# Second part's weight operands made in the products' ring of buffers, and first attention blocks with two rounds between scores and transposes

## The chip, the core and the metric

The kernel runs on one core of a Trainium2 chip. TensorE multiplies matrices into PSUM, VectorE (DVE), ScalarE (ACT) and GpSimd (POOL) work elementwise, and SyncE (SP) issues nearly all DMAs from one queue in order. Every engine runs its own instructions in order and waits on semaphores. The metric is the device time of one execution in microseconds; lower is better.

## What is computed

The data are fp32, except the second part's weights, which come in 64 bits and are turned to fp32 by the kernel. Attention over chunks of 64 tokens is followed by a mixture of four dense two-layer networks weighted by domain probabilities, and that by a gated layer. From the reference:

```python
scores = scale * np.matmul(q_c, k_c.transpose(0, 1, 2, 4, 3))
attn = softmax(scores)                       # per chunk of 64; 4 x 8 heads x 576 tokens x 64
x = heads side by side                       # 2304 tokens x 512
for e in range(4):                           # first part ("one"), w1 512x1024, w2 1024x512
    out += p[:, e:e + 1] * (np.maximum(x @ w1[e], 0.0) @ w2[e])
g = x @ w_gate                               # second part ("two"), 512x1536
return (g * (1 / (1 + np.exp(-g))) * (x @ w_val)) @ w_out
```

## The kernel before

**Split operands.** Each fp32 operand is kept as a high half, rounded by ScalarE, and a low half, the difference, made by VectorE or GpSimd (`split`). A product is three matmuls: high by high, high by low, low by high.

**Sets and products.** Layer 1 is cut into *sets*: a pair of 128-wide weight blocks in each direction against a pass of 768 tokens, done with seven products instead of eight (`PRODUCTS`, `product`). The seven products need sums of weight blocks (`w_sums`, four sums) and sums of x blocks. There are 48 sets of the first part (three passes of 16), then 36 of the second. The counter `now` counts products; one product is a *slot*. A slot holds six matmuls of layer 1 and the share of layer 2 of the group before (`layer2`, `gather` adds the result in VectorE). Three accumulators x, z and w are used: the products 0, 2, 4 and 6 add into x, and ScalarE copies the intermediate state out as `p` (after product 0) and `u` (after product 2) before the next product may add (`keep`).

**Weights of the first part.** Sets 2 to 17 split their operands from raw weights (`make_w`) into a ring of twelve buffers, pool `w`, and store them; later passes load them seven slots ahead (`load_w`).

**Weights of the second part.** While the first part's sets 18 to 47 run, generators make the second part's operands and store them in DRAM: `make_set64` converts two halves of a set (`convert`, from 64 bits to fp32: a ScalarE step `top`, six VectorE steps, one add of GpSimd, spread over slots by `yield`), makes the four sums in VectorE and splits seven operands, one a slot, into pool `made`, which has two buffers. `make_wo` does one block of the output weights. `run_tasks(2)` steps two generators once in a slot; the list `make64` gives two sets, then two blocks of output weights, and so on. A split's store is put off by two slots (`later(2, ...)`). The order of instructions is the order in which the code issues them.

**Opening.** Six blocks of attention run through four stages (scores, transpose, values, out), one block a round, each stage one round behind the one before. The first two sets are done as eight plain pieces (`plain`) between the last rounds and after them; `first_sums` makes the sums of x, `make_w` the operands of set 2, `split_w2` those of layer 2.

Of the kernel before, what the change touches and what calls it, by code (L numbers as in the profile page):

```python
# [10 lines left out]
F32 = mybir.dt.float32  # L11
# [8 lines left out]
P = 128  # L20
B, H, S, D = 4, 8, 576, 64
CH = 64
# [50 lines left out]
def attention_moe_gated(  # L73
# [141 lines left out]
    def att_scores(a, where):  # L215
        s = att[a]
        ps = att_ps(f"s{a}", where)
        for i in range(NPAIR):
            for c in range(2):
                b = slice(64 * c, 64 * c + 64)  # L220
                nc.tensor.matmul(
                    ps[b, 2 * i : 2 * i + 2], s["q"][:, i, b], s["k"][:, :, i, c], start=True, stop=True
                )
        if a + 2 < NS:
            att_load(a + 2)
        mx = st_p.tile([P, H], F32, tag="mx", name=f"mx{a}")
        e = s["e"] = at_p.tile([P, H, CH], F32, tag="e", name=f"e{a}", bufs=3)
        nc.vector.tensor_reduce(out=mx, in_=ps, op=ALU.max, axis=AX.X)
        nc.vector.tensor_tensor(out=e, in0=ps, in1=mx.unsqueeze(2).to_broadcast(ps.shape), op=ALU.subtract)
        nc.scalar.activation(e, e, AF.Exp, scale=SCALE)  # L230
# [40 lines left out]
    def att_out(a, where):  # L271
        ps = transpose(att_ps(f"xt{a}", where), att.pop(a)["e"]).rearrange("p (i c) k -> p i (c k)", c=2)
        s, b = divmod(a, BLOCKS)
        half, b = divmod(b, HALF)
        if s == 0:


            r = slice(b * P, (b + 1) * P)
            ops = [x_slots(0, f"b{i + 1}1") if half == 0 else x_slots(0, ("t4", "b22")[i]) for i in range(2)]
            for i, (h, _) in enumerate(ops):  # L280
                nc.scalar.activation(h[:, :, r], ps[:, 2 * i : 2 * i + 2], AF.Copy)
            for i, (h, l) in enumerate(ops):
                sub(l[:, :, r], ps[:, 2 * i : 2 * i + 2], h[:, :, r].bitcast(F32))
            t = x_first[half, b] = acc_p.tile([P, KD, P], F32, tag="acc", name=f"x0_{a}")
            nc.scalar.copy(t, ps)
        else:
            xb = at_p.tile([P, NPAIR, P], F32, tag="xb", name=f"xb{a}", bufs=1)
            nc.scalar.copy(xb, ps)
            nc.sync.dma_start(xs[s][half, :, :, b * P : (b + 1) * P], xb)

    def first_sums(j):

        b1, b2 = x_first[0, j], x_first[1, j]
        t = raw2_p.tile([P, KD, P], F32, tag="raw2", name=f"t12_{j}")
        r = slice(j * P, (j + 1) * P)
        d0, d1 = slice(0, 2), slice(2, 4)

        def part(b, src, lo=None):
            h, l = x_slots(0, b)
            split(h[:, :, r], l[:, :, r], src, lo)  # L300

        sub(t[:, d0], b2[:, d0], b1[:, d0])
        sub(t[:, d1], b2[:, d1], t[:, d0])
        sub(b2[:, d0], b2[:, d1], b2[:, d0], nc.gpsimd)
        part("t2", t[:, d1])
        part("t1", t[:, d0])
        part("t3", b2[:, d0], nc.gpsimd)
        sub(b1[:, d1], b1[:, d1], t[:, d1], nc.gpsimd)
# [67 lines left out]
    def make_set64(q, m):  # L376
        r = raw1_p.tile([P, 8, 2 * P], F32, tag="raw1", name=f"raw_{q}_{m}")
        for half in range(2):
            dst = r[:, 2 * half : 2 * half + 2].rearrange("p b f -> p (b f)")
            yield from convert(dst, (wg, wv)[m][q, half], f"{q}_{m}_{half}")  # L380
        w_sums(r)
        yield
        for i in range(NPROD):
            a = PRODUCTS[i][1]
            t = made_p.tile([P, 2, 2 * P], F32R, tag="made", name=f"made_{q}_{m}_{a}")
            split(t[:, 0], t[:, 1], r[:, a], lo=nc.gpsimd)
            later(2, lambda i=i, t=t: nc.sync.dma_start(w_d[NPAIRS + 2 * q + m][i], t.bitcast(F32)))
            yield

    def make_wo(c):  # L390
        t = made_p.tile([P, 512], F32, tag="made", name=f"made_wo_{c}")
        yield from convert(t, wo[c], f"wo_{c}")
        yield
        nc.sync.dma_start(wo_d[c], t)
        yield
# [177 lines left out]
    with tc.manual_schedule():  # L573
# [32 lines left out]

        spare = [(psA, "a"), (psA, "a"), (psX, "x"), (psX, "x"), (psY, "y"), (psY, "y")]
        count = [0]  # L610

        def where():
# [2 lines left out]

        ORDER = (A11, A12, A21, A22)
        pieces = [(n, c, t) for t in range(2) for n in range(2) for c in range(2)]
        zw = ("z", "w")
        for i in range(BLOCKS + len(STAGES) - 1):
            for d, stage in reversed(list(enumerate(STAGES))):  # L620
                if 0 <= i - d < BLOCKS:
                    stage(i - d, where())
            if i == 1:
                fetch_w1(1)
            if i in (2, 3):
                for a in ORDER[2 * i - 4 : 2 * i - 2]:
                    wplain[0, a] = w_split(raw1[0], a, 0)
            if i in (4, 5):
                for a in ORDER[2 * i - 8 : 2 * i - 6]:
                    wplain[1, a] = w_split(raw1[1], a, 1)  # L630
            if i >= BLOCKS - 1:
                plain(*pieces.pop(0), zw[i % 2])
            if i == BLOCKS:
                fetch_w2(0, 0)
                fetch_w2(0, 1)

        sm = t_p.tile([P, NS], F32, tag="sum", name="prob_sum", bufs=3)
        nc.vector.tensor_reduce(out=sm, in_=prob, op=ALU.add, axis=AX.X)
        nc.vector.tensor_scalar_add(sm, sm, EPS)
        nc.vector.reciprocal(sm, sm)  # L640
        nc.vector.tensor_tensor(out=prob, in0=prob, in1=sm.unsqueeze(2).to_broadcast(prob.shape), op=ALU.mult)
        raw1.clear()
        fetch_w1(2)
        fetch_w1(3)
        split_w2(0, 0)
        split_w2(0, 1)
        fetch_w2(0, 2)
        fetch_w2(0, 3)
        split_w2(0, 2)
        split_w2(0, 3)  # L650
        plain(*pieces.pop(0), "z")
        first_sums(0)
        w_sums(raw1[2])
        make_w(2, 0)
        plain(*pieces.pop(0), "w")
        first_sums(1)
        make_w(2, 1)
        plain(*pieces.pop(0), "z")
        first_sums(2)
        make_w(2, 2)  # L660
        plain(*pieces.pop(0), "w")
        for i in range(3, NPROD):
            make_w(2, i)
        for j in range(HALF):
            first_last(j)


        rest = []
# [7 lines left out]

        make64 = []
        for q in range(NPAIRS2):
            make64 += [make_set64(q, 0), make_set64(q, 1), make_wo(2 * q), make_wo(2 * q + 1)]

        def run_tasks(n):
            while len(running) < n and tasks:
# [10 lines left out]
        for n in range(FIRST, len(sets)):  # L693
# [3 lines left out]
            if group_of(n) != G:  # L697
# [1 line left out]
                first = now[0]  # L699
                slots = NPROD * sum(group_of(k) == G for k in range(len(sets)))  # L700
                two, taken = layer2(G - 1), 0
            if n + 2 < len(sets) and n + 2 > 3 and is_raw(n + 2):
                fetch_w1(n + 2)
            if n == N1:
                assert not tasks and not running, (len(tasks), len(running))
# [2 lines left out]
            for i in range(NPROD):  # L708
# [29 lines left out]
                if rest and i % 3 != 2:  # L738
                    stage, a = rest.pop(0)
                    stage(a, (psA, "a"))  # L740
                    if not rest:
# [1 line left out]
                        xt_p = ctx.enter_context(tc.tile_pool(name="xt", bufs=3, side="right"))  # L743
                        sums_p = ctx.enter_context(tc.tile_pool(name="sums", bufs=1, side="right"))
                        raw64_p = ctx.enter_context(tc.tile_pool(name="raw64", bufs=2, side="right"))
                        made_p = ctx.enter_context(tc.tile_pool(name="made", bufs=2, side="right"))
                        tasks.append(x_sums(1))
                if n == NPAIRS + 1 and i == NPROD - 1:
                    tasks += [x_sums(2)] + make64
# [73 lines left out]
```

## Time and profile before

| | |
|---|---|
| median of three runs | 1353.57 us (1349.45 to 1357.07) |
| the profiled execution: time, span | 1354.29 us, 1352.5 us |
| TensorE busy | 1281.5 us (95%) |
| VectorE, ScalarE, GpSimd busy | 754.3, 516.8, 551.7 us |
| mean granted TensorE clock | 0.981 |

An engine's busy time in a stretch is less than the stretch when it waited; "idle before" names what ended the wait. The granted clock is 1 at 2.4 GHz and 0.5 at 1.2 GHz, so 0.97 is a mean over both levels. A matmul's own duration overlaps the next one's, so the distance between starts is its cost.

### The profile page before, as it was taken

The page shows a single profiled execution, that of the slowest core. Times are in us where ns is not written, and L with a number is a line of the kernel's source. Part 1 is how long each engine was busy: PE and PEld are TensorE (multiplying, and loading weights), DVE is VectorE, ACT ScalarE, POOL GpSimd, SP SyncE. Part 2 cuts the span into 40 slices and gives each one's busy share as a digit, 9 for nine tenths or more (in the row PEclk, how much of TensorE's full clock was granted, in tenths as well). Part 3 has the DMA queues.
Part 4 walks back from the last instruction along what each step waited for, and adds up shares of the span by engine and source line. Part 5 has one row for each costly group of instructions (what it writes and reads, how often), then busy time and mean ns, then how long its engine had stood idle before and what let it go on. Part 6 is the DMA issues. An engine that isn't in the chain of part 4 may idle for free.

```text
span 1352.5 us, 19817 instructions
## 1 busy us (share of the span) xinstructions
PE 1281.5 (95%) x6724; PEld 1141.2 (84%) x6724; DVE 754.3 (56%) x1246; ACT 516.8 (38%) x1105; POOL 551.7 (41%) x527
## 2 busy tenths in 40 slices
PE   7899999999999989889898888999999999999998
PEld 6788888888987879778797777889999899989997
DVE  5665555556467867678458366544435433453343
ACT  3544444445433333343332333243334333343331
POOL 2543343567353353453443335242536323252331
PEclk9899999999999999999999898999999999999999
DMA  6286676676886767686884755665887666567651
GB/s 203 79 265 219 205 217 193 209 243 221 258 279 225 250 222 261 198 285 239 278 295 158 246 193 201 231 228 173 279 271 241 217 226 202 168 226 250 187 170 47
DMA packets 166885, 296.16 MB, mean 219 GB/s; under 512 B 17776, under 2 KB 43632, under 8 KB 166784
## 3 DMA queue, kind: packets, MB, share of 16 engines
q1 hardware_dynamic: 166752, 294.85, 65.7%
q8 instruction: 54, 0.88, 0.3%
q14 instruction: 47, 0.39, 0.1%
q0 software_dynamic: 32, 0.04, 0.0%
HBM read 219.84 MB, written 74.97 MB: 218 GB/s over the span
## 4 chain that ended last, share of the span: by engine, by line
PE 37%; DMA 7%; DVE 7%; issue 3%; ACT 3%; POOL 2%; SPq 0%; ACTq 0%; DVEq 0%; POOLq 0%
PE y L521 5%; PE y L517 5%; PE y L519 5%; PE lx L470 4%; PE lx L472 4%; PE lx L471 4%; DMA w<-made 4%; PE lz L470 2%; PE lz L471 2%; PE lz L472 2%; POOL made L106 1%; PE lw L472 1%; PE lw L471 1%; PE lw L470 1%; DMA raw_wo<-wo 1%
## 5 line engine op out<-in xcount | busy, mean ns | idle before, releaser
L106 POOL TENSOR_TENSOR w<-raw,w 128x512 fp32r<-128x512 f32 (+1 forms) x252 | 270.8, 1089 | 488.9 <-ACT w L105 418.2
L517 PE MATMUL y<-w,hh 128*128 128x512 f32 x792 | 315.5, 398 | 15.2 <-DVE acc L545 13.8
L521 PE MATMUL y<-w,hl 128*128 128x512 f32 x792 | 315.9, 399 | 2.3 <-DVE hl L428 2.3
L519 PE MATMUL y<-w,hh 128*128 128x512 f32 x792 | 314.8, 397 | 0.0
L517 PEld LDWEIGHTS y<-w,hh 128*128 128x128 f32 x792 | 150.6, 190 | 37.3 <-DVE acc L545 18.6
L521 PEld LDWEIGHTS y<-w,hl 128*128 128x128 f32 x792 | 150.9, 191 | 23.1 <-DVE hl L428 2.7
L519 PEld LDWEIGHTS y<-w,hh 128*128 128x128 f32 x792 | 150.4, 190 | 17.3
L105 ACT ACTIVATE w<-raw 128x512 fp32r<-128x512 f32 (+1 forms) x252 | 124.8, 522 | 11.2 <-DMA raw<-w 11.2
L458 DVE TENSOR_TENSOR sum_p<-lw,p 128x384 f32<-128x384 f32 x82 | 45.5, 555 | 149.3 <-PE lw L472 133.2
L427 ACT ACTIVATE hh<-sum_p 128x384 fp32r<-128x384 f32 x92 | 48.1, 523 | 193.2 <-DVE sum_p L458 193.0
L458 DVE TENSOR_TENSOR sum_p<-lx,p 128x384 f32<-128x384 f32 x82 | 45.5, 555 | 135.8 <-PE lx L472 121.8
L109 POOL TENSOR_TENSOR hl<-sg,hh 128x384 fp32r<-128x384 f32 x72 | 74.1, 1034 | 97.1 <-ACT hh L445 65.7
L428 DVE SCALAR_TENSOR_TENSOR hl<-sum_p,hh 128x384 fp32r<-128x384 f32 x92 | 60.1, 654 | 74.2 <-ACT hh L427 74.2
L545 DVE SCALAR_TENSOR_TENSOR acc<-y,prob,acc 128x512 f32<-128x512 f32 x126 | 93.7, 744 | 11.1 <-PE y L521 10.5
L106 POOL TENSOR_TENSOR made<-raw,made 128x256 fp32r<-128x256 f32 x84 | 64.9, 782 | 81.6 <-ACT made L105 76.4
L454 ACT COPY u<-lx 128x384 f32<-128x384 f32 x82 | 38.9, 474 | 100.4 <-PE lx L472 100.3
L470 PE MATMUL lx<-t2h,w 128*128 128x384 f32 x164 | 59.3, 362 | 17.8 <-ACT p L454 17.7
L470 PE MATMUL lx<-t3h,w 128*128 128x384 f32 x164 | 58.3, 355 | 14.1 <-ACT u L454 14.0
L454 ACT COPY p<-lx 128x384 f32<-128x384 f32 x82 | 39.0, 475 | 85.3 <-PE lx L472 85.0
L331 DVE TENSOR_TENSOR raw<-raw 128x256 f32<-128x256 f32 x112 | 65.6, 627 | 3.5 <-POOL raw L373 2.6
L105 ACT ACTIVATE made<-raw 128x256 fp32r<-128x256 f32 x84 | 34.5, 415 | 74.4 <-DMA w<-made 71.6
L470 PE MATMUL lx<-t4h,w 128*128 128x384 f32 x164 | 56.4, 344 | 2.7 <-DVE sum_p L458 2.6
(199 smaller groups left out, 2774.1 us busy)
## 6 DMA issues: line engine op xcount, KB each, us to landing
w<-w SPq DMA_DIRECT2D x574, 256.0 KB, 4.3
raw<-w SPq DMA_DIRECT2D x96, 256.0 KB, 4.3
w<-made SPq DMA_DIRECT2D x84, 256.0 KB, 2.1
raw<-w SPq DMA_DIRECT2D x18, 512.0 KB, 4.2
raw<-wo SPq DMA_DIRECT2D x36, 256.0 KB, 2.9
b<-x SPq DMA_DIRECT2D x40, 192.0 KB, 3.3
xt<-b SPq DMA_DIRECT2D x40, 192.0 KB, 3.8
xraw_t<-xt SPq DMA_DIRECT2D x20, 384.0 KB, 3.5
```

The source lines that it names most:

```text
L105: nc.scalar.activation(h, src, AF.Copy)
L106: (lo or nc.vector).tensor_tensor(out=l, in0=src, in1=h.bitcast(F32), op=ALU.subtract)
L109: (eng or nc.vector).tensor_tensor(out=o, in0=a, in1=b, op=ALU.subtract)
L454: nc.scalar.copy(t, ps)
L458: nc.vector.tensor_tensor(out=t, in0=ps, in1=snap.pop(name), op=ALU.add)
L470: nc.tensor.matmul(ps, w[:, 0, c], xh[:, k], start=f, stop=False, skip_group_check=True)
L471: nc.tensor.matmul(ps, w[:, 0, c], xl[:, k], start=False, stop=False, skip_group_check=True)
L472: nc.tensor.matmul(ps, w[:, 1, c], xh[:, k], start=False, stop=e, skip_group_check=True)
L517: nc.tensor.matmul(y, hh[:, c], w[:, 0], start=(j == 0), stop=False)
L519: nc.tensor.matmul(y, hh[:, c], w[:, 1], start=False, stop=False)
L521: nc.tensor.matmul(y, hl[:, c], w[:, 0], start=False, stop=(j == 3))
L545: nc.vector.scalar_tensor_tensor(out=sum_, in0=y, scalar=p, in1=sum_, op0=ALU.mult, op1=ALU.add)
```

## The change

Two things are changed. First, `make_set64` takes its seven tiles from the ring of pool `w` (through `w_split`, as the first part does), the pool `made` is gone, and the block of output weights has two buffers of its own. The list of tasks gives one set, then one block of output weights. One more `yield` stands before the sums of a set. Second, in the opening the scores run two rounds ahead of the transposes, the exponentials use accumulator buffers, GpSimd takes the low halves of four of the six blocks from the copy in SBUF and the sums of set 2's weights, and the steps after the last round are put in another order: sums of x and operands of set 2 stand between the plain pieces, layer 2's operands between them.

```diff
@@ att_scores
-        e = s["e"] = at_p.tile([P, H, CH], F32, tag="e", name=f"e{a}", bufs=3)
+        pool, how = (acc_p, dict(tag="acc")) if a < BLOCKS else (at_p, dict(tag="e", bufs=3))
+        e = s["e"] = pool.tile([P, H, CH], F32, name=f"e{a}", **how)
@@ att_out
-            for i, (h, l) in enumerate(ops):
-                sub(l[:, :, r], ps[:, 2 * i : 2 * i + 2], h[:, :, r].bitcast(F32))
             t = x_first[half, b] = acc_p.tile([P, KD, P], F32, tag="acc", name=f"x0_{a}")
             nc.scalar.copy(t, ps)
+            src, eng = (ps, nc.vector) if b == HALF - 1 else (t, nc.gpsimd)
+            for i, (h, l) in enumerate(ops):
+                sub(l[:, :, r], src[:, 2 * i : 2 * i + 2], h[:, :, r].bitcast(F32), eng)
@@ first_sums
-        t = raw2_p.tile([P, KD, P], F32, tag="raw2", name=f"t12_{j}")
+        t = acc_p.tile([P, KD, P], F32, tag="acc", name=f"t12_{j}")
@@ make_set64
+        yield
         w_sums(r)
         yield
         for i in range(NPROD):
             a = PRODUCTS[i][1]
-            t = made_p.tile([P, 2, 2 * P], F32R, tag="made", name=f"made_{q}_{m}_{a}")
-            split(t[:, 0], t[:, 1], r[:, a], lo=nc.gpsimd)
+            t = w_split(r, a, f"made_{q}_{m}")
@@ make_wo
-        t = made_p.tile([P, 512], F32, tag="made", name=f"made_wo_{c}")
+        t = raw64_p.tile([P, 512], F32, tag="made", name=f"made_wo_{c}")
@@ the opening
-        spare = [(psA, "a"), (psA, "a"), (psX, "x"), (psX, "x"), (psY, "y"), (psY, "y")]
+        spare = [(psA, "a"), (psX, "x"), (psY, "y")]
...
+        LAGS = ((att_out, 4), (att_scores, 0), (att_values, 3), (att_turn, 2))
+        for i in range(BLOCKS + 4):
+            for stage, lag in LAGS:
+                if 0 <= i - lag < BLOCKS:
+                    stage(i - lag, where())
...
+            if i >= HALF + 3:
+                plain(*pieces.pop(0), "zw"[i % 2])
+            if i == 9:
+                w_sums(raw1[2], nc.gpsimd)
...
+        plain(*pieces.pop(0), "x")
+        first_sums(0)
+        make_w(2, 0)
+        split_w2(0, 0)
+        plain(*pieces.pop(0), "x")
+        first_sums(1)
+        make_w(2, 1)
+        split_w2(0, 1)
...
+        plain(*pieces.pop(0), "z")
+        first_sums(2)
+        make_w(2, 2)
+        plain(*pieces.pop(0), "w")
+        make_w(2, 3)
+        split_w2(0, 2)
+        make_w(2, 4)
+        split_w2(0, 3)
...
@@ the tasks
-            make64 += [make_set64(q, 0), make_set64(q, 1), make_wo(2 * q), make_wo(2 * q + 1)]
+            for m in range(2):
+                make64 += [make_set64(q, m), make_wo(2 * q + m)]
```

**The order on TensorE, opening.** `s` is the scores of a block, `et` the transposed exponentials, `av` the values, `xt` the output turned. Of before, behind the warm-up:

```order
L221 MATMUL s_198<-kbd_158,q_183 64x128 x8
L234 MATMUL et_216<-ident,e_212 128x128 x4
L221 MATMUL s_228<-kbd_159,q_187 64x128 x8
L258 MATMUL av_248<-vbd_160,et_221 64x128 x8
L234 MATMUL et_260<-ident,e_242 128x128 x4
L221 MATMUL s_272<-kbd_158,q_207 64x128 x8
L234 MATMUL xt_296<-ident,e_212 128x128 x4
L258 MATMUL av_311<-vbd_161,et_265 64x128 x8
```

Of the change, at the same place:

```order
L221 MATMUL s_198<-kbd_158,q_183 64x128 x8
L221 MATMUL s_216<-kbd_159,q_187 64x128 x8
L221 MATMUL s_234<-kbd_158,q_207 64x128 x8
L235 MATMUL et_252<-ident,e_212 128x128 x4
L221 MATMUL s_270<-kbd_159,q_225 64x128 x8
L259 MATMUL av_288<-vbd_160,et_257 64x128 x8
L235 MATMUL et_300<-ident,e_230 128x128 x4
L235 MATMUL xt_320<-ident,e_212 128x128 x4
```

Three blocks' scores now stand ahead of the first transposes.

**The order on GpSimd, behind the plain pieces.** `x` is an operand of attention, `t3l` the low half of a sum of x, `w_1` and the like an operand of set 2, `w_0_0` and the like an operand of layer 2 (128x512). Of before:

```order
L106 TENSOR_TENSOR w_0_0_631<-raw_0_0_550,w_0_0_631 128x512
L106 TENSOR_TENSOR w_0_1_634<-raw_0_1_552,w_0_1_634 128x512
L106 TENSOR_TENSOR w_0_2_641<-raw_0_2_637,w_0_2_641 128x512
L106 TENSOR_TENSOR w_0_3_644<-raw_0_3_639,w_0_3_644 128x512
L109 TENSOR_TENSOR x_3_507<-x_3_507 128x256
L106 TENSOR_TENSOR t3l_677<-x_3_507,t3h_676 128x2x128
L109 TENSOR_TENSOR x_0_309<-x_0_309,t_0_664 128x256
L106 TENSOR_TENSOR w_1_685<-raw_2_627,w_1_685 128x256
```

Of the change, the end of that stretch:

```order
L109 TENSOR_TENSOR x_5_603<-x_5_603 128x256
L106 TENSOR_TENSOR t3l_660<-x_5_603,t3h_659 128x2x128
L109 TENSOR_TENSOR x_2_443<-x_2_443,t_2_725 128x256
L106 TENSOR_TENSOR w_5_736<-raw_2_477,w_5_736 128x256
L106 TENSOR_TENSOR w_4_756<-raw_2_477,w_4_756 128x256
L106 TENSOR_TENSOR w_0_2_759<-raw_0_2_704,w_0_2_759 128x512
L106 TENSOR_TENSOR w_6_762<-raw_2_477,w_6_762 128x256
L106 TENSOR_TENSOR w_0_3_765<-raw_0_3_706,w_0_3_765 128x512
```

Layer 2's four operands stood ahead of the three rounds of sums; now the last two stand behind them.

**The order on ScalarE, while set 25 of the first part runs.** `made_0` and `made_1` are the tiles of two sets of the second part, `p` and `u` the copies out of the accumulators, `hh` the high half of a hidden tile, `w_12_2` an operand of layer 2. Of before:

```order
L105 ACTIVATE made_0_4_5311<-raw_0_4925 128x256
L105 ACTIVATE made_1_1_5314<-raw_1_4993 128x256
L454 COPY p_25_5324<-lz_5317 128x384
L105 ACTIVATE made_0_6_5334<-raw_0_4925 128x256
L105 ACTIVATE made_1_2_5337<-raw_1_4993 128x256
L427 ACTIVATE hh_3_1_5348<-sum_p_25_5346 128x384
L105 ACTIVATE made_0_7_5363<-raw_0_4925 128x256
L105 ACTIVATE made_1_5_5366<-raw_1_4993 128x256
```

Of the change:

```order
L456 COPY p_25_5240<-lx_5233 128x384
L105 ACTIVATE w_made_0_4_5251<-raw_0_4831 128x256
L429 ACTIVATE hh_2_0_5263<-sum_p_25_5261 128x384
L105 ACTIVATE w_made_0_6_5275<-raw_0_4831 128x256
L456 COPY u_5285<-lx_5233 128x384
L105 ACTIVATE w_12_2_5292<-raw_12_2_5221 128x512
L105 ACTIVATE w_made_0_7_5302<-raw_0_4831 128x256
L456 COPY p_25_5312<-lz_5305 128x384
```

The splits of two sets alternated between the copies; now those of one set do.

## Rows read from the trace of the kernel before

**Rows 1.** Busy time by stretch; columns: stretch, length, each engine's busy time, granted clock, DMA, GB/s.

```profile
0.00:61.00 61.00, 46.21 (x353) 40.21 (x354) 36.94 (x76) 25.36 (x58) 20.52 (x31) 0.92 0.52 156
380.00:880.00 500.00, 454.90 (x2149) 398.12 (x2148) 330.06 (x533) 174.04 (x377) 208.50 (x189) 0.97 0.69 235
```

**Rows 2.** Timeline of TensorE, starts of sets: start, duration (us), instruction.

```profile
375.36 0.33 PE L470 MATMUL lx<-b11h,w 128*128 128x384 f32 x1
...
530.45 0.33 PE L470 MATMUL lx<-b11h,w 128*128 128x384 f32 x1
...
546.20 0.33 PE L470 MATMUL lx<-b11h,w 128*128 128x384 f32 x1
...
903.56 0.33 PE L470 MATMUL lx<-b11h,w 128*128 128x384 f32 x1
```

**Rows 3.** Waits of TensorE, 380 to 880 us: waited for, total, times, longest.

```profile
PE lx L470 <- ACT u L454: 14.0, 10, 3.1
PE y L517 <- DVE acc L545: 12.7, 7, 3.8
PE lx L470 <- ACT p L454: 11.6, 8, 3.3
```

**Rows 4.** Waits of ScalarE in the same stretch.

```profile
ACT made L105 <- DMA w<-made: 71.6, 52, 3.8
```

**Rows 5.** Timeline of ScalarE at 647 us; in brackets the idle time before.

```profile
647.19 0.42 ACT L105 ACTIVATE made<-raw 128x256 fp32r<-128x256 f32 x1 [3.81 <-DMA w<-made]
```

**Rows 6.** Timeline of VectorE at 817 to 826 us.

```profile
817.04 0.69 DVE L369 SCALAR_TENSOR_TENSOR raw<-raw 128x512 f32<-128x512 uint32 x1
...
818.10 1.70 DVE L369 SCALAR_TENSOR_TENSOR raw<-raw 128x512 f32<-128x512 uint32 x1
...
821.54 5.05 DVE L331 TENSOR_TENSOR raw<-raw 128x256 f32<-128x256 f32 x8
```

**Rows 7.** Timeline of TensorE at two stops.

```profile
597.79 0.50 PE L517 MATMUL y<-w,hh 128*128 128x512 f32 x1 [1.98 <-DVE acc L545]
...
610.77 0.44 PE L470 MATMUL lx<-t2h,w 128*128 128x384 f32 x1 [3.35 <-ACT p L454]
```

**Rows 8.** DMA issues by line: number, KB each, us from issue to landing.

```profile
w<-w SPq DMA_DIRECT2D x574, 256.0 KB, 4.3
...
w<-made SPq DMA_DIRECT2D x84, 256.0 KB, 2.1
```

**Rows 9.** Timeline of TensorE in the opening.

```profile
5.42 1.93 PE L221 MATMUL s<-kbd,q 128*64 128x128 f32 x16 [0.26 <-DMA kbd<-kt]
...
23.29 0.66 PE L234 MATMUL et<-ident,e 128*128 128x128 f32 x4 [1.30 <-ACT e L230]
...
23.88 1.09 PE L221 MATMUL s<-kbd,q 128*64 128x128 f32 x16
...
47.16 0.33 PE L470 MATMUL plw<-t4h,w 128*128 128x384 f32 x1
...
49.07 0.34 PE L472 MATMUL plw<-b22h,w 128*128 128x384 f32 x1
...
60.73 0.52 PE L470 MATMUL lx<-b11h,w 128*128 128x384 f32 x1
...
68.35 0.39 PE L519 MATMUL y<-w,hh 128*128 128x512 f32 x1
```

**Rows 10.** Timeline of GpSimd in the opening.

```profile
44.89 2.54 POOL L106 TENSOR_TENSOR w<-raw,w 128x512 fp32r<-128x512 f32 x2 [8.78 <-ACT w L105]
...
57.81 0.98 POOL L109 TENSOR_TENSOR x<-x 128x256 f32<-128x256 f32 x1 [1.16 <-DVE t L109]
...
61.59 0.92 POOL L109 TENSOR_TENSOR x<-x 128x256 f32<-128x256 f32 x1
```

**Rows 11.** Busy time, 800 to 825 us, columns as in the first group.

```profile
800.00:825.00 25.00, 22.93 (x111) 19.68 (x110) 21.67 (x33) 7.87 (x17) 11.63 (x9) 1.00 0.49 161
```

**Rows 12.** Waits of SyncE's queue, 380 to 880 us.

```profile
SPq L387 <- POOL made L106: 115.0, 77, 8.9
```

More of the change, by code (lines that the diff above doesn't have):

```diff
@@ L617, in attention_moe_gated, with w_plain @@
         pieces = [(n, c, t) for t in range(2) for n in range(2) for c in range(2)]
[L618 to L623, printed above, removed]
-                fetch_w1(1)
[L625 to L633, printed above, removed]
+        def w_plain(n, some):
+            for a in some:
+                wplain[n, a] = w_split(raw1[n], a, n)
+        LAGS = ((att_out, 4), (att_scores, 0), (att_values, 3), (att_turn, 2))
[3 more added lines that the diff above has]
+                    stage(i - lag, where())
+            if i == 2:
+                w_plain(0, ORDER[:2])
+            elif i == 3:
+                w_plain(0, ORDER[2:])
+                fetch_w1(1)
+            elif i == 5:
+                w_plain(1, ORDER[:2])
+            elif i == 6:
+                w_plain(1, ORDER[2:])
+                fetch_w1(2)
+            elif i == 7:
                 fetch_w2(0, 0)
                 fetch_w2(0, 1)
+            if i >= HALF + 3:
+                plain(*pieces.pop(0), "zw"[i % 2])
+            if i == 9:
+                w_sums(raw1[2], nc.gpsimd)
+        del raw1[0], raw1[1]
+        fetch_w1(3)
+        plain(*pieces.pop(0), "x")
[6 more added lines that the diff above has]
+        split_w2(0, 1)
+        fetch_w2(0, 2)
+        fetch_w2(0, 3)
+        plain(*pieces.pop(0), "z")
[6 more added lines that the diff above has]
+        split_w2(0, 3)
+        for j in range(HALF):
+            first_last(j)
+        make_w(2, 5)
+        make_w(2, 6)
         sm = t_p.tile([P, NS], F32, tag="sum", name="prob_sum", bufs=3)
@@ L641, in attention_moe_gated @@
         nc.vector.tensor_tensor(out=prob, in0=prob, in1=sm.unsqueeze(2).to_broadcast(prob.shape), op=ALU.mult)
[L642 to L665, printed above, removed]
         rest = []
@@ L701, in attention_moe_gated @@
                 two, taken = layer2(G - 1), 0
-            if n + 2 < len(sets) and n + 2 > 3 and is_raw(n + 2):
+            if n + 2 > 3 and is_raw(n + 2):
                 fetch_w1(n + 2)
@@ L745, in attention_moe_gated @@
                         raw64_p = ctx.enter_context(tc.tile_pool(name="raw64", bufs=2, side="right"))
-                        made_p = ctx.enter_context(tc.tile_pool(name="made", bufs=2, side="right"))
                         tasks.append(x_sums(1))
```

## Prediction

> **What bounds the kernel now.** I read the stretches first. From 380 to 880 us TensorE is busy 454.90 of 500 us, so 45.1 us are idle, and its granted clock is 0.97 of full; the opening 61 us are the other poor stretch, 46.21 us busy [rows 1]. These two are where the change is made: the first is where the weight operands of the second part are made beside the products of the first, the second is the attention of the first six blocks.
>
> The price of the first stretch is better read from the starts of the sets. A set (seven products and its share of layer 2) starts with a product on b11h. Where nothing disturbs it a set takes 546.20 - 530.45 = 15.75 us; from 375.36 to 903.56 there are 29 sets in 528.20 us [rows 2]. Undisturbed they would be 29 x 15.75 = 456.8 us, and six turns of finished blocks lie among them, at 0.66 us each as four transposes take it in [rows 9], 4.0 us. So 528.2 - 456.8 - 4.0 = **67.4 us** are lost. 45.1 of these are idle time; the granted clock of 0.97 is 0.03 x 500 = 15 us more; the rest, some 7 us, is first matmuls after a stop. A microsecond of idle time costs 67.4 / 45.1 = 1.5 us here.
>
> Then the waits of that stretch. TensorE waited 14.0 us for the copy u, 11.6 us for the copy p, both ScalarE's, and 12.7 us for the accumulation in VectorE [rows 3]. ScalarE's copies are late because it runs in order and stands in front of a split whose buffer is still being stored: 71.6 us in 52 waits on the store of an earlier made tile, up to 3.8 us [rows 4]. At 647.19 one such wait took 3.81 us [rows 5]; a copy p or u stands right behind such a split in ScalarE's order, and a product in the same accumulator waits for that copy. VectorE's lateness has the other cause: two sets run in step, so both sets' sums stand in a row, eight instructions in 5.05 us [rows 6].
>
> **The change part by part.** *Made tiles in the ring of twelve.* Before, a made tile has two buffers; its store is issued two slots (products) after the split, so a third split finds a store that was issued in the slot before or in the same one, seldom two before. A store lands 2.1 us after issue [rows 8] and a slot is 15.75 / 7 = 2.25 us, so the wait is built in. In the changed program 84 splits take a buffer of the ring whose last user was a product one to six slots earlier, or a store issued two to five slots earlier. Two slots are 4.5 us against 2.1, so the 71.6 us go nearly whole. ScalarE does the same 84 splits: no instruction is added.
>
> The ring also takes something away. With a set being made, up to three of the twelve buffers hold made tiles, and a product's load finds a buffer later freed. It is issued seven slots, 15.75 us, ahead of its product and lands in 4.3 us [rows 8], so 11.4 us are spare; a load that waits for a store waits for one issued two to seven slots ago. I price this at nothing; the cover is those 11.4 us on SyncE's queue, and the last rival prices its loss.
>
> *One set at a time, each with one block of the output weights.* VectorE, GpSimd and DMA work is the same. What changes is that the eight sums in a row become four (about 2.5 us), two blocks of output weights are no longer converted side by side, and the splits of two sets no longer alternate. The extra pause before the sums gives GpSimd's add one slot more. A coincidence remains: at five places the four sums stand in one slot with another conversion step, or next to it. With about 1 us of ordinary VectorE work per slot that is some 5 us in 2.25 us, a lateness near 3 us, where u and p tolerate about two slots.
>
> *What stays.* Two stops, 1.98 us and 3.35 us, lie at the change of pass, where the x operands are split as well [rows 7]; the change does not touch them. I keep these 5.3 us, and take another 5 us for five coincidences at 1 us each. Residual idle 10.5 us, at 1.5 us each 16 us. **Gain 67.4 - 16 = 51.5 us.** Ends: all of it (67.4), or half the idle time staying (22.5 x 1.5 = 34, gain 33).
>
> *The opening.* The scores now run two rounds ahead of the transposes, so a round's transposes no longer wait for the exponential of the same round (1.30 us in [rows 9]). TensorE's own list is six blocks at 0.66 + 1.09 + 1.09 + 0.66 = 3.5 us (scores as values, out as transposes), 21 us, and eight plain pieces of 49.07 + 0.17 - 47.16 = 2.1 us, 17 us. From the first scores at 5.42 this ends at 43.4 if it never waits. It does wait: the third block's scores for their reload, and each round for a copy behind the exponential; following the instructions by hand I put the first product of set 2 at **48.4** instead of 60.73. Before, a set's first 7.6 us lead from there to the first use of the low half of layer 2's fourth operand, at 68.35 [rows 9]; so 56.0 would be the best.
>
> But that operand is now made late, in GpSimd's queue. The sums of the t operands start when the fifth plain piece is drained, at about 44.1. GpSimd then has three rounds of about 61.59 - 57.81 = 3.8 us [rows 10], four low halves of layer 2 at 2.54 / 2 = 1.27 us, and two more weight splits of about 0.9: 11.4 + 5.1 + 1.8 = 18.3 us, so the fourth operand is there at 62.4. TensorE reaches the mark of 68.35 at 62.4: 6 us sooner, less 1 us for a slower clock after the stop. **Gain 5 us**, ends 0 (GpSimd beside a busy VectorE as slow as its slowest rows) and 11 (TensorE's own list). Moving eight low halves and four sums from VectorE to GpSimd is in this: before 44.1 GpSimd has room. The exponentials and the t operands now take accumulator buffers; each is given out after its last reader, which stands well ahead in the order, so I price that at nothing (its cover is the same order; lost, it would be one read of 0.98 us [rows 10] each).
>
> Elsewhere nothing changes; the second part, from 903.56 on, keeps its order.
>
> **A rule of the Trainium skill against it.** At 818.10 a VectorE instruction that takes 0.69 us alone took 1.70 us, beside a GpSimd add [rows 6]. The Trainium skill (SBUF — State Buffer, "Who interferes with whom") has it that VectorE instructions with two SBUF inputs or in a two-port mode and GpSimd's share one port pair, as an exclusive lock: the second to come is blocked outright. By that rule the same locking work has to fit into a shorter stretch, and the lateness of VectorE grows; it is the second case below, and the rows above bear it out in size at single places.
>
> **The rivals.** *Forecast:* 1354.3 - 51.5 - 5 = 1297.8 us for the execution shown (span 1352.5, 1.8 us around it). It is 0.7 above the median of the runs, so 1297.
>
> *VectorE becomes the bound.* It is busy 330.06 of 500 us [rows 1]; in 440 us that is 75%. For it: from 800 to 825, with VectorE busy 21.67 of 25 us, TensorE was idle 2.07 us [rows 11], at 1.5 that is 12%. If half the stretch went like that, 228 x 0.12 / 0.88 = 31 us stay, and with the 8 us of pass changes the gain is 28 + 4: 1322 us. Against it: the sets at 530 and 546 ran clean while two sets were converted, staggered [rows 2]. 1312 to 1340.
>
> *Clean:* all stops but the pass changes go and the opening gains 9 us: 1354.3 - 67.4 + 8 - 9 = 1286, down to 1278 if these go too.
>
> *Nothing in the main stretch:* splits that wait for products as long as they waited for stores. 1354 - 5 = 1349. Against it: those products are issued a slot or more earlier, and TensorE runs ahead of ScalarE.
>
> *Slower: loads come late.* SyncE's queue runs in order. It waited 115.0 us on GpSimd for made tiles, up to 8.9 us at once [rows 12]. Made stores and loads now share buffers, so a load can stand behind a store that stands behind GpSimd. From 11.4 us of lateness on, products wait for weights. If half of the 29 x 7 = 203 products then waited 1 us, at 1.5, that is 152 us: 1354 - 56 + 152 = 1450. Against it: 8.9 is under 11.4, and with one set at a time GpSimd's queue is shorter.
>
> **How the numbers follow.** Forecast (1285 to 1312) 0.58; VectorE bound 0.20; clean 0.12; nothing 0.05; slower 0.05. The range reaches from the clean case to the middle of the VectorE case: 1279 to 1328. Faster by over 0.5%, which is about what a measurement here can tell, holds for the first three, 0.9, and the case of nothing (1349 is 0.3%) gives 0.05 for the same.
>
> **What would show it.** ScalarE's waits on stores of made tiles should fall from 71.6 us to under 5. Sets between the same two marks should mostly take 15.75 us, with long ones at the pass changes, and the granted clock should be 0.99 or more there. The first product of set 2 should start near 48 us, with a stop of several microseconds for layer 2's low halves on GpSimd behind it. The forecast is wrong if TensorE waits for loads, if VectorE's waits replace ScalarE's, or if the opening only moves its waiting behind 48 us.

## The result, and the profile after

The changed kernel takes 1299.85 us (median, 1296.29 to 1303.07); its ratio to the kernel before is 0.9604, 95% interval 0.9558 to 0.965. One of the four executions of the kernel before took 7019.23 us and is left out. The profiled execution has a span of 1297.9 us against 1352.5: 54.6 us less. The forecast was 1297, range 1279 to 1328, so the time is where it was put. The two terms of the sum came out differently, though, and the experiments below show that much of the reason given for the larger one was wrong.

First the stretches, as in [rows 1] (stretch, length, busy time of TensorE, its weight loads, VectorE, ScalarE, GpSimd, granted clock, DMA share, GB/s). The main stretch comes earlier now, so its window does too.

```profile
0.00:53.00 53.00, 42.23 (x355) 37.80 (x356) 27.82 (x56) 21.84 (x50) 21.77 (x36) 0.94 0.57 170
380.00:830.00 450.00, 442.69 (x2187) 396.03 (x2186) 330.41 (x538) 175.55 (x381) 210.53 (x190) 1.00 0.76 261
```

TensorE is idle 7.3 us of 450 where it was idle 45.1 of 500, and the granted clock is 1.00 instead of 0.97. VectorE does the work of [rows 1] in 450 us: 330.41 / 450 = 73% busy, nearly the 75% feared, and TensorE waits for it no more than the lines below show. In the chain that ended last TensorE has 81% of the span, against 37% before.

The starts of the 29 sets of [rows 2], in TensorE's timeline:

```profile
378.66 0.33 PE L472 MATMUL lx<-b11h,w 128*128 128x384 f32 x1
...
848.95 0.33 PE L472 MATMUL lx<-b11h,w 128*128 128x384 f32 x1
```

That is 848.95 - 378.66 = 470.29 us against 528.20. Counted as in the prediction, 470.29 - 456.8 - 4.0 = 9.5 us are lost, not 67.4: **57.9 us gained** in the main stretch. The first of these sets begins 3.3 us later than before (378.66 against 375.36), and the part behind the last is unchanged (448.95 against 448.94). 57.9 - 3.3 = 54.6, the whole difference: in these two executions the new opening gains nothing and costs 3.3 us.

The waits that answer to [rows 3, 4], from 380 to 830 us (waited for, total, times, longest), TensorE's and then ScalarE's on made tiles:

```profile
PE lx L472 <- ACT u L456: 2.1, 1, 2.1
PE lx L472 <- ACT p L456: 1.6, 1, 1.6
PE y L519 <- DMA w<-w_made: 1.4, 1, 1.4
PE y L519 <- DVE acc L547: 1.0, 1, 1.0
```

```profile
ACT w_made L105 <- DMA w<-w_made: 1.3, 1, 1.3
```

All that is left for p and u stands at the change of pass, where [rows 7] had its stops:

```profile
591.80 0.44 PE L472 MATMUL lx<-t2h,w 128*128 128x384 f32 x1 [1.64 <-ACT p L456]
594.53 0.50 PE L519 MATMUL y<-w,hh 128*128 128x512 f32 x1 [0.96 <-DVE acc L547]
599.84 0.44 PE L472 MATMUL lx<-t3h,w 128*128 128x384 f32 x1 [2.14 <-ACT u L456]
```

The wait of 1.4 us put down to a store is VectorE's. It is in layer 2, whose operands do not lie in the ring, and TensorE goes on 0.05 us after an accumulation ends (748.65 + 0.74) that stood in VectorE behind four sums and two steps of a conversion:

```profile
749.44 0.50 PE L519 MATMUL y<-w,hh 128*128 128x512 f32 x1 [1.41 <-DMA w<-w_made]
```

```profile
744.48 3.18 DVE L333 TENSOR_TENSOR raw<-raw 128x256 f32<-128x256 f32 x4
...
748.65 0.74 DVE L547 SCALAR_TENSOR_TENSOR acc<-y,prob,acc 128x512 f32<-128x512 f32 x1
```

### The profile page after: what moved, and what is told of

It reads as the page before. It is cut to its first block, busy times and chain, and to the rows that moved or that the text cites. A ratio compares the mean times of both kernels' runs of the same rounds, so it can differ in the third digit from the quotient of the medians.

```text
span 1297.9 us, 19723 instructions
## 1 busy us (share of the span) xinstructions
PE 1260.3 (97%) x6724; PEld 1131.5 (87%) x6724; DVE 745.7 (57%) x1234; ACT 514.8 (40%) x1105; POOL 561.0 (43%) x539
## 4 chain that ended last, share of the span: by engine, by line
PE 81%; DMA 6%; DVE 5%; ACT 2%; issue 2%; SPq 2%; POOL 1%; DVEq 0%; POOLq 0%; ACTq 0%
PE y L521 12%; PE y L523 12%; PE y L519 12%; PE lx L472 8%; PE lx L473 8%; PE lx L474 8%; PE lz L472 4%; PE lz L473 4%; PE lz L474 4%; PE lw L472 2%; PE lw L473 2%; PE lw L474 2%; DMA xraw_t<-xt 1%; PE av L259 1%; DMA raw<-w 1%
## 5 line engine op out<-in xcount | busy, mean ns | idle before, releaser
L519 PEld LDWEIGHTS y<-w,hh 128*128 128x128 f32 x792 | 149.1, 188 | 25.1 <-DVE acc L547 6.0
L521 PEld LDWEIGHTS y<-w,hh 128*128 128x128 f32 x792 | 148.9, 188 | 20.5 <-POOL w L106 3.6
L106 POOL TENSOR_TENSOR w_made<-raw,w_made 128x256 fp32r<-128x256 f32 x84 | 69.1, 832 | 50.2 <-ACT w_made L105 47.3
L456 ACT COPY p<-lx 128x384 f32<-128x384 f32 x82 | 39.0, 475 | 89.9 <-PE lx L474 89.6
L333 DVE TENSOR_TENSOR raw<-raw 128x256 f32<-128x256 f32 x108 | 61.8, 612 | 0.9
L456 ACT COPY p<-lz 128x384 f32<-128x384 f32 x82 | 39.3, 479 | 49.3 <-PE lz L474 48.5
L472 PE MATMUL lz<-b22h,w 128*128 128x384 f32 x164 | 57.1, 348 | 0.0
```

Source lines behind the costliest of these rows:

```text
L106: (lo or nc.vector).tensor_tensor(out=l, in0=src, in1=h.bitcast(F32), op=ALU.subtract)
L472: nc.tensor.matmul(ps, w[:, 0, c], xh[:, k], start=f, stop=False, skip_group_check=True)
L519: nc.tensor.matmul(y, hh[:, c], w[:, 0], start=(j == 0), stop=False)
L521: nc.tensor.matmul(y, hh[:, c], w[:, 1], start=False, stop=False)
```

## Experiments: which half of the main change did it

For the runs below two marks are read from each profile: the *excess* of the 29 sets of the main stretch (length - 456.8 - 4.0, as above), and the start of set 5 (set 2 begins behind the opening, sets 3 and 4 follow), which shows the opening. Ratios are to the kernel before, run beside it on the same chip; kernels named together in a section were not always on one chip, so I compare ratios, not medians.

| kernel | median us | ratio (95%) | excess us | set 5 at us |
|---|---|---|---|---|
| before | 1353.57 | 1 | 67.4 | 121.10 |
| changed | 1299.85 | 0.9604 (0.9558 to 0.965) | 9.5 | 123.90 |
| changed, once more | 1297.33 | 0.9537 (0.9505 to 0.957) | 8.2 | 123.13 |
| main change alone | 1296.58 | 0.9549 (0.9521 to 0.9576) | 7.4 | 121.95 |
| ring alone | 1334.97 | 0.983 (0.9794 to 0.9865) | 50.8 | 121.89 |
| order alone | 1310.4 | 0.965 (0.9622 to 0.9678) | 25.4 | 121.32 |
| ring, second set four slots later | 1309.98 | 0.965 (0.9621 to 0.9679) | 24.2 | 122.71 |
| changed, no pause | 1305.97 | 0.961 (0.9591 to 0.9629) | 15.2 | 123.47 |
| changed, sums twice | 1310.64 | 0.9641 (0.9606 to 0.9675) | 21.8 | 124.66 |
| opening alone | 1361.36 | 1.0009 (0.9991 to 1.0028) | 67.0 | 123.39 |
| changed, raw block of set 4 later | 1295.05 | 0.9527 (0.9497 to 0.9557) | 9.1 | 119.38 |
| changed, layer-2 splits earlier | 1299.57 | 0.9565 (0.9539 to 0.9591) | 8.1 | 125.15 |
| both of these | 1294.02 | 0.9524 (0.9499 to 0.9548) | 8.0 | 119.40 |
| both, banks swapped | 1297.08 | 0.954 (0.9517 to 0.9563) | 7.5 | 120.99 |

The theory behind the prediction (A): TensorE stops for p and u because ScalarE stands on the stores of made tiles. The rival (B): two sets made in step crowd VectorE, and ScalarE behind it.

**The main change alone**: the kernel before with the edits of `make_set64`, `make_wo` and the task list.

> The second part's operands made in the ring, one set at a time, with the opening of before. If the two parts of the change act apart: sets start at 375.4 as before and the main stretch lasts 470.3 us as after, the second part 448.9; span 375.4 + 470.3 + 448.9 = 1294.6, time 1296, some 3 us under the changed kernel. If the new opening gives the main stretch something (a better clock, transfers already out), the stretch is longer than 470 here and the time is 1300 or more.

Span 1294.6, excess 7.4, second part as before. The two parts act apart, and the main change without the new opening can't be told from the whole (0.9549 against 0.9604 and, measured again, 0.9537).

**Ring alone.**

```diff
@@ make_set64 (of before)
-            t = made_p.tile([P, 2, 2 * P], F32R, tag="made", name=f"made_{q}_{m}_{a}")
-            split(t[:, 0], t[:, 1], r[:, a], lo=nc.gpsimd)
+            t = w_split(r, a, f"made_{q}_{m}")
@@ make_wo
-        t = made_p.tile([P, 512], F32, tag="made", name=f"made_wo_{c}")
+        t = raw64_p.tile([P, 512], F32, tag="made", name=f"made_wo_{c}")
```

> Ring alone, two sets still made in step. Theory A, the stores of made tiles held ScalarE up: its waits on stores fall from 71.6 us to under 5, TensorE's waits for the copies u and p (25.6 us) nearly go, those for the accumulation (12.7 us) stay; idle time in the main stretch falls from 45 to about 16 us, time near 1354 - 1.5 x 27 = 1313. Theory B, it is the two sets in step that crowd VectorE and ScalarE: less than 15 us gained, 1340 or more.

Neither: 1335. The waits on stores go as A said, but 50.8 us of excess stay. (The profiled execution took 1340.85 us, the longest of four; at the median it would be some 45.) ScalarE's waits on made stores, then TensorE's waits, 380 to 880 us:

```profile
ACT w_made L105 <- DMA w<-w_made: 3.2, 3, 2.0
```

```profile
PE y L516 <- DVE acc L544: 15.1, 7, 4.7
PE lx L469 <- ACT u L453: 6.8, 6, 2.5
PE lx L469 <- DVE sum_p L457: 4.4, 3, 1.9
PE lx L469 <- ACT p L453: 3.1, 3, 1.8
```

The copy u is still late, and two stops show how. In the timelines (start, duration, instruction, in brackets the idle time before and what ended it) TensorE at 849.85 waited 2.51 us for u; ScalarE had stood 8.28 us in front of `hh`, which waits for VectorE's `sum_p`, with u behind it in its order; and VectorE could not make `sum_p` before 848.33, since it did two conversions, each step twice, in a row (one step is shown twice, and the last):

```profile
849.85 0.44 PE L469 MATMUL lx<-t3h,w 128*128 128x384 f32 x1 [2.51 <-ACT u L453]
```

```profile
848.91 0.52 ACT L426 ACTIVATE hh<-sum_p 128x384 fp32r<-128x384 f32 x1 [8.28 <-DVE sum_p L457]
849.34 0.46 ACT L453 COPY u<-lx 128x384 f32<-128x384 f32 x1
```

```profile
842.75 0.69 DVE L364 TENSOR_TENSOR top_wo<-top_wo,raw_wo 128x512 int32<-128x512 int32 x1
...
844.62 0.69 DVE L364 TENSOR_TENSOR top_wo<-top_wo,raw_wo 128x512 int32<-128x512 int32 x1
...
846.75 1.66 DVE L369 SCALAR_TENSOR_TENSOR raw_wo<-raw_wo 128x512 f32<-128x512 uint32 x1
848.33 0.55 DVE L457 TENSOR_TENSOR sum_p<-lw,p 128x384 f32<-128x384 f32 x1
```

At 815.45 TensorE waited 4.73 us for the accumulation, which stood in VectorE behind eight sums in a row, as in [rows 6]:

```profile
815.45 0.80 PE L516 MATMUL y<-w,hh 128*128 128x512 f32 x1 [4.73 <-DVE acc L544]
```

```profile
808.75 5.98 DVE L331 TENSOR_TENSOR raw<-raw 128x256 f32<-128x256 f32 x8
814.66 0.74 DVE L544 SCALAR_TENSOR_TENSOR acc<-y,prob,acc 128x512 f32<-128x512 f32 x1
```

**Order alone**: the pool `made` of two buffers stays.

```diff
@@ make_set64 (of before)
+        yield
         w_sums(r)
@@ the task list
-            make64 += [make_set64(q, 0), make_set64(q, 1), make_wo(2 * q), make_wo(2 * q + 1)]
+            for m in range(2):
+                make64 += [make_set64(q, m), make_wo(2 * q + m)]
```

> One set at a time alone, the two made buffers kept. Theory A: one split a slot still meets a store issued in the same slot, so ScalarE's waits on stores stay at 50 us or more and most of TensorE's waits for u and p stay: 1325 to 1345. Theory B: the waits for the accumulation go and with them the stops for u and p, since two splits never stand in one slot: 1300 to 1310.

1310.4: B's number. And yet the waits that A blamed are nearly all still there, ScalarE's waits from 380 to 860 us:

```profile
ACT made L105 <- DMA w<-made: 68.4, 32, 4.1
```

while TensorE waits little for what stands behind them (5.1 + 3.6 + 2.2 us for p and u, against 25.6 in [rows 3]):

```profile
PE lx L471 <- ACT p L455: 5.1, 3, 2.6
PE lz L471 <- ACT p L455: 3.6, 4, 1.2
...
PE lx L471 <- ACT u L455: 2.2, 3, 1.4
```

So those 68 us of waiting cost no more than about the 14 us that the ring still adds to the order (0.965 to 0.9549 of 1354 us; each ratio is known to some 4 us). Theory A as I held it falls. The ring alone is worth 23 us by its ratio and 14 beside the order; the order, here always with the pause before the sums, is worth 47 alone and 38 beside the ring.

**The same ring with the second set of a pair four slots later.** It asks whether it is the coincidence or the number of sets alive that costs.

```diff
@@ the task list (ring alone)
-            make64 += [make_set64(q, 0), make_set64(q, 1), make_wo(2 * q), make_wo(2 * q + 1)]
+            make64 += [make_set64(q, 0), waits(4, make_set64(q, 1)), make_wo(2 * q), make_wo(2 * q + 1)]
```

(`waits` yields that often, then runs the task.)

> The ring with the tasks in the order of before (both sets of a pair, then two blocks of output weights), but the second set of a pair begins four slots after the first. It still has two sets alive at once. If coincidence of the same steps is what costs (both conversions, both rows of sums in one slot), the eight sums in a row become twice four and the stops of 2 to 5 us on VectorE go: 1297 to 1305, close to the ring with one set at a time (1296.6). If two sets alive at once cost by their mere amount of work, little changes against the ring alone: 1325 to 1335.

1309.98, somewhat above the first case: 0.983 becomes 0.965, 24 of the 38 us that the whole order brings beside the ring. With the same sets alive and the same work, four slots of stagger do most of it, so coincidence is the larger cause. TensorE's waits for the accumulation are 6.3 us instead of 15.1. This run lacks the pause too, which by the next one is worth some 6 to 9 of the 14 us that are left.

**Without the pause.**

```diff
@@ make_set64 (of the changed kernel)
-        yield
         w_sums(r)
```

> The changed kernel without the pause ahead of the sums. If the pause only gives GpSimd's add a slot, VectorE stands before it for at most one add (1.4 us) at 12 sets and TensorE has slack for that: within 2 us of the changed kernel. If the pause is what keeps the sums and a conversion step out of one slot, stops of 2 to 3 us come back at several of the 12: 1310 or more.

Between the two cases: the excess is 15.2 us, 6 to 7 over the changed kernel's two profiles, and the median 8.6 over that of the changed kernel on the same chip. No stop comes back at most sets; single ones of 0.3 to 3.5 us do. The pause had one sentence and no price in the prediction.

**Sums made twice.**

```diff
@@ make_set64 (of the changed kernel)
         w_sums(r)
+        w_sums(r)
```

> The changed kernel with the four sums of each of the second part's 12 sets made twice, so that eight stand in a row again on VectorE (the second four repeat the first). Theory L: rows of VectorE work longer than a slot are what stopped TensorE, stores or not. Then stops of 2 to 5 us return at most of the 12 sets, though no wait on a store does: 12 x 3 us x 1.5 = 54 us at most, half of it if every second row finds slack, so 1315 to 1350. Rival: a row of eight hurt only together with the waits on stores or with two conversions side by side: under 1305.

Again between: 1310.64, excess 12 to 14 us more than the changed kernel's, and of the stops one is of the size expected, at 759.11:

```profile
759.11 0.80 PE L520 MATMUL y<-w,hh 128*128 128x512 f32 x1 [4.05 <-DVE acc L548]
```

```profile
752.68 4.64 DVE L333 TENSOR_TENSOR raw<-raw 128x256 f32<-128x256 f32 x8
```

Eight sums in a row stop TensorE without any wait on a store, but at a few of the twelve sets only, where an accumulation is due. The stop at 759.11 is at the place where the changed kernel stops for 1.41 us as well (749.44 above), with two steps of a conversion between the sums and the accumulation. Such rows are a part of what the two sets in step cost, not the whole; the conversions side by side, as at 842 us above, are another. I have not split the rest further.

## Experiments: what the opening did

**The new opening alone**: the changed kernel with the main change undone.

> The new opening alone, the main stretch as before. If the opening costs 3 us wherever it stands, the set that started at 375.4 starts at 378.7 and the time is 1357, 0.2% over the kernel before, inside what the runs can tell. The forecast on record had it 5 us faster, 1349. The stop of 3.6 us near 88 us should be there, behind a wait of ScalarE for a layer-2 load.

1.0009 (0.9991 to 1.0028): no gain and no loss that the runs can tell, and not the 5 us forecast. The traces tell a little more. With the old opening set 5 starts at 121.10, 121.95, 121.89, 121.32 and 122.71 in five profiles, with the new one at 123.90, 123.13, 123.39, 123.47 and 124.66: 1.9 us later in the mean. By the start of the main stretch the two overlap (375.36 to 378.31 and 376.94 to 378.69), so the 3.3 us of the first two profiles are more than the usual. The stop near 88 us is there, 1.97 us long, behind a wait of ScalarE of 6.05 us for a layer-2 load. The profile of the changed kernel shows where the gain goes. TensorE:

```profile
52.64 0.33 PE L472 MATMUL lx<-b11h,w 128*128 128x384 f32 x1
...
58.16 0.57 PE L521 MATMUL y<-w,hh 128*128 128x512 f32 x1 [2.26 <-POOL w L106]
...
65.95 0.39 PE L521 MATMUL y<-w,hh 128*128 128x512 f32 x1
...
87.69 1.09 PE L221 MATMUL s<-kbd,q 128*64 128x128 f32 x16 [3.58 <-ACT et L246]
```

Set 2 starts 8.1 us sooner than in [rows 9] and reaches the mark of 68.35 (first use of the fourth layer-2 operand's low half) at 65.95, 2.4 us sooner. At 87.69 that is lost again: the scores wait for a bank whose copy `et` is late in ScalarE, which had waited twice for a layer-2 load:

```profile
78.63 0.94 ACT L105 ACTIVATE w<-raw 128x512 fp32r<-128x512 f32 x2 [4.59 <-DMA raw<-w]
...
85.62 1.55 ACT L105 ACTIVATE w<-raw 128x512 fp32r<-128x512 f32 x4 [4.96 <-DMA raw<-w]
87.08 0.56 ACT L246 COPY et<-et 128x512 f32<-128x512 f32 x1
```

Those loads (L405) stood in SyncE's queue. It issued nothing from 53.21 + 5.25 = 58.5 to 70.09, where the raw block of set 4 (L324) goes out, whose buffer GpSimd's last split of set 2 has to free; then seven stores came ahead of the second load:

```profile
70.09 0.33 SPq L324 DMA_DIRECT2D raw<-w  x1
...
72.15 0.53 SPq L405 DMA_DIRECT2D raw<-w  x1
72.73 5.00 SPq L343 DMA_DIRECT2D w<-w  x7
...
80.50 0.51 SPq L405 DMA_DIRECT2D raw<-w  x1
```

In the kernel before that fetch goes out 2.1 us sooner:

```profile
68.01 0.33 SPq L322 DMA_DIRECT2D raw<-w  x1
```

The new order itself puts it off: on GpSimd the three low halves of t4 now stand ahead of the last two splits of set 2, where they stood behind them. Before, then after:

```profile
67.94 2.82 POOL L106 TENSOR_TENSOR t4l<-x,t4h 128x256 fp32r<-128x256 f32 x3
```

```profile
65.49 2.82 POOL L106 TENSOR_TENSOR t4l<-x,t4h 128x256 fp32r<-128x256 f32 x3
68.27 3.17 POOL L106 TENSOR_TENSOR w<-raw,w 128x256 fp32r<-128x256 f32 x4
```

The first two of these four splits are set 2's; they end at 70.06.

Behind the stop at 87.69 the granted clock is 0.53 from 89 to 92.2, which is the 1.2 GHz level, so set 3 takes 24.67 us where it took 19.47:

```profile
89.00:92.20 3.20, 3.20 (x11) 2.81 (x11) 2.93 (x7) 0.17 (x1) 0.66 (x1) 0.53 0.40 69
```

The other four profiles with this opening have the same stop, of 1.22 to 2.84 us. In them set 3 starts later (80.49 to 82.15, against 78.99) and the scores at 88.45 to 88.78, so the loads set this time, and not how early set 3 began.

**The raw block of set 4 fetched later.**

```diff
@@ the loop over sets
-            if n + 2 > 3 and is_raw(n + 2):
+            if n + 2 > 4 and is_raw(n + 2):
                 fetch_w1(n + 2)
...
                 product(n, i)
+                if n == 2 and i == 3:
+                    fetch_w1(4)
```

> The changed kernel, with the raw block of set 4 fetched after the fourth product of set 2 instead of ahead of the first. Theory S: SyncE's queue stood from 58.5 to 70.1 us behind that fetch, and the layer-2 loads behind it came too late. Then the first of these loads is issued some 6 us sooner, ScalarE's waits of 4.59 and 4.96 us for such loads fall under 2, the stop of 3.58 us near 88 and the 4 us of half clock behind it go; set 4 starts near 98.5 instead of 103.7, time 1295. Rival: the loads are slow because of the seven stores of 256 KB beside them; then the stop stays and the time is 1300.

SyncE issues the first load at 63.15 and the second at 72.77; ScalarE waits for neither, the stop is gone, and set 3 takes 19.47 us again:

```profile
63.15 0.33 SPq L405 DMA_DIRECT2D raw<-w  x1
63.52 6.40 SPq L343 DMA_DIRECT2D w<-w  x7
69.98 0.42 SPq L324 DMA_DIRECT2D raw<-w  x1
...
72.77 0.58 SPq L405 DMA_DIRECT2D raw<-w  x1
```

The time is 1295.05, as Theory S has it. The first load lands 2.9 us after its issue with the seven stores right behind it, the second after 5.4, where the changed kernel's took 6.5 and 5.1; so it was the queue, and not the stores beside the loads. Set 5 starts at 119.38, 3.8 to 4.5 us sooner than in the changed kernel's two profiles.

**Layer-2 splits earlier** (the same lines are gone from behind `make_w(2, 0)` and `make_w(2, 1)`).

```diff
@@ the opening (of the changed kernel)
         plain(*pieces.pop(0), "x")
+        split_w2(0, 0)
+        split_w2(0, 1)
+        fetch_w2(0, 2)
+        fetch_w2(0, 3)
         first_sums(0)
         make_w(2, 0)
```

> The changed kernel, with the first two layer-2 operands split ahead of the sums of the t operands, where GpSimd stands idle for 3.97 us. The stops of 2.26 and 0.61 us on GpSimd at 58 and 64 us go, and the half clock from 58.7 to 61.9: set 3 starts 4 to 5 us sooner, at 74 to 75. If SyncE's queue is what makes the later stop (Theory S), most of this is given back there, as GpSimd's last split comes only 2.6 us sooner: set 4 at 100 to 102, time 1297. If not, all is kept: set 4 at 99, time 1295.

Missed: set 3 starts at 80.57, set 4 at 104.91, and the time is 1299.57. The stops on GpSimd's layer-2 halves go, and others take their place: 1.18 us on GpSimd's half for the first product and 3.17 us on VectorE's `hl`: the last plain piece's drain, in the accumulator that the second product of set 2 needs.

**Both edits.**

> Both edits on the changed kernel. Theory S: set 3 at 74 to 75, set 4 at 94 to 95, time 1290 to 1291. If loads are slow by the stores beside them: set 4 near 99, time 1295.

Missed as well: set 3 at 79.69, set 4 at 99.16, 1294.02, which is what the first edit gave, and nothing from the second. These are the numbers of the case of slow loads, but not by its cause: ScalarE waits 0.4 us for a load from 62 to 100 us, and set 3 is late by the same wait on `hl` (3.18 us at 61.42).

**Both, with the accumulators of the last two plain pieces swapped**, so that the second product need not wait for that drain.

```diff
@@ the opening
-        plain(*pieces.pop(0), "z")
+        plain(*pieces.pop(0), "w")
         first_sums(2)
         make_w(2, 2)
-        plain(*pieces.pop(0), "w")
+        plain(*pieces.pop(0), "z")
```

> The kernel with both edits, the last two plain pieces with their accumulators swapped (w, then z). There TensorE stood 3.18 us at 61.4 before the second product of set 2, whose accumulator w was the last plain piece's; that piece's drain stands behind the last sums of the t operands. If that is the cause, the wait goes and the next one is for the low half of that product's weights, ready at 58.7: 2 to 3 us sooner, 1291 to 1292. If GpSimd's next low halves bind anyway, nothing is gained: 1294.

The wait of 3.18 us goes and two others come, 1.65 us at 60.79 and 2.10 us at 63.38, for layer 2's operands in ScalarE and GpSimd. Set 3 starts at 81.29 and the time is 1297.08: neither case.

In the nine profiles with the new opening or a version of it, set 3 starts between 78.99 and 82.15, and at 81.39 in the kernel before: TensorE reaches set 2 sooner by 6 to 9 us in each, and each time something made by ScalarE, VectorE or GpSimd was not ready. Whether GpSimd's list alone sets that end was not tried.

**The changed kernel once more**, beside the last two.

> The changed kernel once more, to stand beside the two others on one chip: ratio to the kernel before 0.957 to 0.960, span 1298, and the stop of 3.6 us near 88 us again.

Ratio 0.9537, under the range expected, and the stop near 88 again, with 1.22 us. The two measurements of one kernel, 0.9604 and 0.9537, lie 9 us apart, though the kernel itself took 1299.85 and 1297.33: it is the kernel before that took 1353.57 us beside the first and 1358.28 to 1359.54 beside all the others. That says what a difference of 4 us means here: the versions with the later fetch are ahead of the changed kernel by their marks and their medians, 1294.02 and 1295.05, but their intervals and the changed kernel's second one overlap.

## Why the prediction was right, and where it was wrong

**The main stretch: right in size, wrong in its reason.** 57.9 us against 51.5, inside 33 to 67.4; the residue is 9.5 us instead of 16. The stops at the change of pass stayed, as forecast: 1.64 + 0.96 + 2.14 = 4.7 us against 5.3. Of the five coincidences, 5 us, little came: from 380 to 830 us all other idle time is 7.3 - 4.7 = 2.6 us, and 1.4 of it, at 749.44, is such a coincidence. The step that failed is the one that turns 71.6 us of ScalarE's waits on stores [rows 4] into TensorE's waits for p and u [rows 3]. The rows did not show that: they show both, and one place [rows 5] where they stand in line. The order alone keeps 68.4 us of those waits and still gains 47 us; the ring alone takes them away and gains 23. VectorE's burden stood in the text as a cause of the 12.7 us for the accumulation; it is also, through ScalarE's `hh` in front of u, a cause of those for u. The sum held because both halves of the change were in it and the forecast was made for the whole excess, not half by half.

**The ring's price.** No product of the main stretch waited for a load or a store; the 1.4 us put down to one were VectorE's. Made stores now land in 3.5 us instead of 2.1 [rows 8] and loads in 4.5 instead of 4.3; the 4.5 us of two slots still cover that. The rival of late loads did not come.

**VectorE as the bound.** Not at 73% busy. The rule cited for it can be seen once more in the ring alone at 587.49: a VectorE `tensor_scalar`, which has one input, takes 2.08 us beside a GpSimd subtraction that ends at 589.28, and 0.42 us elsewhere, as at 842.29.

```profile
587.49 2.08 DVE L363 TENSOR_SCALAR raw_wo<-raw_wo 128x512 int32<-128x512 int32 x1
...
842.29 0.42 DVE L363 TENSOR_SCALAR raw_wo<-raw_wo 128x512 int32<-128x512 int32 x1
```

```profile
587.26 2.02 POOL L106 TENSOR_TENSOR b11l<-xraw_b,b11h 128x768 fp32r<-128x768 f32 x1 [0.90 <-ACT b11h L105]
```

By the Trainium skill (SBUF — State Buffer, "Who interferes with whom") a `tensor_scalar` can enter a two-port mode, and in such a mode it contends with GpSimd: the second of the two to issue is blocked until the first ends. The trace agrees at this place, where VectorE's instruction starts 0.2 us after GpSimd's and ends 0.3 us after it; that it ran in such a mode no row shows. Such waits make a row in VectorE longer, but by the runs above what decides is whether rows of two sets meet.

**The opening: no gain, and by the marks a small loss.** It was forecast to gain 5 us. The first product of set 2 came at 52.64, not 48.4. The third block's scores waited 5.87 us for their reload, until 14.54, which is later than I had followed by hand:

```profile
14.54 1.97 PE L221 MATMUL s<-kbd,q 128*64 128x128 f32 x16 [5.87 <-DMA kbd<-kt]
```

The rest of the 4 us I have not traced. GpSimd's list was priced well, 18.3 us against 48.16 to 65.53 = 17.4 us, but it began at 48.16 instead of 44.1, so the mark of 68.35 was reached at 65.95 instead of 62.4. Then "elsewhere nothing changes" failed: SyncE's queue was looked at for the main stretch only. It is released by GpSimd's last split of set 2, which the new order puts 2.1 us later (68.01 before, 70.09 after), while TensorE comes sooner, by 8.1 us at set 2 and 2.4 us at set 3, to need the layer-2 loads behind it. The slack that had hidden the queue was spent from both ends. Those last splits ahead of t4's halves were not tried.

## What to carry to other kernels

The total of an engine's waits is no price: some 70 us of ScalarE's waits on stores cost 14 to 23, while two generators in step, which show up as no wait of their own, cost most of the 38 to 47 us that the order is worth. ScalarE's largest wait of all, `hh` for VectorE's `sum_p`, was 139.3 us in the stretch of [rows 4] and is 143.2 us in the changed kernel from 380 to 830. Undo such a change half by half before believing the reason, since a sum made for the whole can be right for the wrong half. And when the bounding engine is moved ahead, look at every in-order queue whose head does not move with it, or moves the other way.

## What the runs showed of the hardware

The seven stores of a set, none of which waited for an engine, take SyncE 5.0 us to issue (72.73 in the changed kernel, 0.7 us each), so a load behind them is issued later by that much. The other unexpected number is the price of one stop for TensorE near 88 us. In the changed kernel 3.58 us idle, with 3.2 us at a granted clock of 0.53 behind them, make set 3 5.2 us longer than 19.47. The same stop is shorter in other profiles. In the opening alone 1.97 us idle cost 2.0 us, and the granted clock from 89.8 to 93.0 is 1.00; in the changed kernel once more 1.22 us cost 1.3, at 1.00 from 89.6 to 92.8. With the sums made twice 2.84 us cost 4.5, at 0.63, a mean over both levels, from 90.0 to 93.2.
